# Changing the queues of the last stores, the prefetch of residual tiles and the start of the first products in a fused transformer block

## The chip, the cores and the metric

The kernel runs on one core of one Trainium2 chip. The metric is the device time of one execution, in microseconds (us). A timed value is that time. The span is the part of it that the profile covers, from the first instruction to the last, and is 1.6 to 2.2 us shorter. "Clock" is the mean clock granted to TensorE, as a share of full speed.

The engines are named as in the profile. PE is TensorE's matrix products and PEld its weight loads. DVE is VectorE, ACT is ScalarE, POOL is GpSimd and SP is SyncE. A "q" after the name means the engine's sequencer, which waits and issues transfers.

## The reference

The kernel computes one transformer block and all its gradients: linear attention (32 heads of 20), then a gated feed-forward network, each with a layer norm ahead and a residual. S is 2048, D 640 and F 1728, all in bf16.

```python
phi = lambda t: jnp.where(t > 0, t + 1, jnp.exp(t)) + 1e-6
q, k, v = ...                     # layernorm(x) @ wqkv, cut into heads
kv  = einsum("bhsd,bhse->bhde", phi(k), v)
z   = einsum("bhsd->bhd", phi(k))
o   = einsum(phi(q), kv) / (einsum(phi(q), z)[..., None] + 1e-6)
h   = x + o.reshape(B, S, D) @ wo
out = h + (silu(ln(h) @ w_gate) * (ln(h) @ w_up)) @ w_down
# returned: out, and the gradients for x, wqkv, wo, w_gate, w_up, w_down
```

## The kernel before

The token axis is cut into 16 tiles of 128 rows. The change touches three places.

**The start.** For every tile, VectorE makes the layer-norm statistics and the normalised tile `xn`. PE transposes that, ScalarE copies it out as `xnT`, PE multiplies it with the weights of k and q, ScalarE takes exp and relu, and VectorE makes phi of them.

```python
nc.sync.dma_start(out=x_tm[0][:, 0, 0:320], in_=x_v[:, 0, 0:320])
nc.scalar.dma_start(out=x_tm[0][:, 0, 320:640], in_=x_v[:, 0, 320:640])
load_x(nc.sync, 1, 2)
nc.sync.dma_start(out=wqk[:, :, D:2 * D], in_=...)       # k weights, one transfer of 800 KB
# after the statistics of tile 0: x tile 2, q weights, x tile 3
...
def kq_phi(t):
    for dst, e, r in ers.pop(t):
        nc.vector.tensor_scalar(out=e, in0=e, scalar1=1.0, scalar2=1e-6, op0=ALU.min, op1=ALU.add)
        nc.vector.tensor_tensor(out=half(dst[:, t, :]), in0=e, in1=r, op=ALU.add)
...
for t in range(ST):
    # t > 0:  normalise tile t+1, then k of tile t
    # t == 0: k of tile 0, then normalise tile 1
    ...                            # statistics of tile t+2
    kq_mm(t, 1)                    # q
    if t > 0:
        kq_phi(t - 1)
```

**The attention output.** Each tile reloads its residual `xr` on SyncE's queue in its own turn. Five transposed blocks of W2 go to memory on GpSimd's queue.

```python
xr = wk("xr")
nc.sync.dma_start(out=xr[:], in_=x_v[:, t, :])
... # products into ps_a, add, statistics, rstd on GpSimd
if 2 <= u <= DT + 1:
    nc.gpsimd.dma_start(out=mat_v(scr_W2T)[:, :, (u - 2) * P:(u - 1) * P], in_=w2t)
```

**The last stage.** Each of 16 tiles loads its `h1` rows on GpSimd's queue, adds the product with w_down, and stores the result on GpSimd's queue. Only the last tile's stores go by SyncE and ScalarE. The V part of the weight gradient (`dwv`, five stores) goes by GpSimd too.

```python
for t in range(ST):
    h1r = wk("h1r")
    nc.gpsimd.dma_start(out=h1r[:], in_=scr_h1_v[:, t, :])
    ...                                   # 28 products into ps_o
    nc.vector.tensor_tensor(out=half(h1r[:]), in0=row(ps), in1=half(h1r[:]), op=ALU.add)
    nc.gpsimd.dma_start(out=o0_v[:, t, :], in_=h1r[:])      # t < 15
    if t < DT:
        dwo(t); tr_sb(dKV, dKVT, t); tr_piece(Y, scr_Yt, t) # transposes on SyncE's queue
    if ST - 1 - DT <= t < ST - 1:
        dwv(t - (ST - 1 - DT))                              # store on GpSimd's queue
```

## Time and profile before

| | kernel before |
|---|---|
| time, median of 6 runs beside the changed kernel | 835.86 us (834.39 to 837.68) |
| profiled span, mean clock | 834.23 us, 0.996 |
| first k product starts | 7.87 us |
| z stage starts (after 16 tiles of k and q) | 57.28 us |
| PE's last product ends | 828.26 us |
| GpSimd's closing DRAIN | 825.47 to 833.45 us |

The table of windows and the timelines are the views that matter, because PE is busy 99% of the span. A part of the change can only be worth what PE stands still for in that place, or what comes after PE's last product. The rows are in the prediction below.

### The profile page before, as it was taken

Reading aid. Unit: us, or ns where it says so; the run is one execution under the profiler, and the core shown is the slowest. Engines: PE = TensorE matmul, PEld = TensorE weight load, DVE = VectorE, ACT = ScalarE, POOL = GpSimd, SP = SyncE. Lnnn points to the kernel's source line nnn. Section 1 sums busy time; section 2 is a strip of 40 time slices with the busy share of each in tenths; the row PEclk is TensorE's granted clock in tenths of the full one; section 3 lists DMA queues with packets and bytes.
Section 4 is the critical chain, followed back from the end, with each engine's and each line's share of the span. In section 5 each row is a group of like instructions: output and inputs, shape, how many; then the busy total and the mean of one; then the engine's idle time right before and its main releaser. Section 6 shows DMA issues by size and latency. Waiting matters only on the chain.

```text
span 834.2 us, 14051 instructions
## 1 busy us (share of the span) xinstructions
PE 823.7 (99%) x5523; PEld 529.3 (63%) x5523; DVE 446.1 (53%) x874; ACT 291.2 (35%) x414; POOL 197.2 (24%) x358
## 2 busy tenths in 40 slices
PE   8999999999999999999999999999999999999997
PEld 6776656555555555555656777777776777777775
DVE  6978757791087028810840158778864366611111
ACT  5983422670184125401830222232322133322000
POOL 2330132322312312221227102121301111112332
PEclk9999999999999999999999999999999999999999
DMA  9995899998559987993697758886698599899952
GB/s 290 184 353 127 166 162 253 278 237 199 145 130 213 211 196 167 202 234 89 123 267 176 248 145 197 198 199 161 165 196 141 106 179 158 158 244 194 278 154 80
DMA packets 277123, 158.55 MB, mean 190 GB/s; under 512 B 235760, under 2 KB 262960, under 8 KB 277056
## 3 DMA queue, kind: packets, MB, share of 16 engines
q1 hardware_dynamic: 250992, 80.48, 52.4%
q0 software_dynamic: 18688, 67.73, 26.6%
q10 hardware_dynamic: 7376, 9.44, 3.8%
q8 instruction: 43, 0.70, 0.4%
q14 instruction: 24, 0.20, 0.1%
HBM read 47.43 MB, written 53.46 MB: 121 GB/s over the span
## 4 chain that ended last, share of the span: by engine, by line
PE 86%; DVE 7%; DMA 3%; SPq 1%; ACT 1%; issue 1%; POOL 0%; ACTq 0%; DVEq 0%; POOLq 0%
PE ps_dw L558 20%; PE ps_dhn L116 14%; PE ps_dxn L792 8%; PE ps_o L845 7%; PE ps_kq L116 5%; PE ps_dwqk L116 5%; PE pg L486 4%; PE pu L491 4%; PE ps_y L116 3%; PE ps_gt L610 3%; PE ps_dk L116 3%; PE ps_dp L116 3%; PE ps_dm L328 2%; PE pdm L328 2%; DMA xr<-in_A_x_dram 1%; DVE m_s L513 1%
## 5 line engine op out<-in xcount | busy, mean ns | idle before, releaser
L116 PE MATMUL ps_dhn<-wgT,cols 128*128 128x320 bf16 x864 | 119.5, 299 | 0.0
L558 PE MATMUL ps_dw<-dd,hn 128*128 128x448 bf16 (+1 forms) x640 | 118.8, 346 | 0.0
L116 PEld LDWEIGHTS <-cols 128*128 128x128 bf16 x864 | 84.5, 98 | 32.9
L558 PEld LDWEIGHTS <-hn 128*128 128x128 bf16 x640 | 62.6, 98 | 54.2
L560 DVE CAST dwev<-ps_dw 128x896 bf16<-128x896 f32 (+3 forms) x12 | 10.9, 908 | 124.0 <-PE ps_dw L558 124.0
L523 POOL DMA_DIRECT2D scr_dT<-stg x64 | 34.7, 542 | 165.8 <-DMA stg<-dd 162.8
L560 ACT CAST dwev<-ps_dw 128x896 bf16<-128x896 f32 (+1 forms) x20 | 17.6, 879 | 158.3 <-PE ps_dw L558 158.3
L135 DVE CUSTOM_DVE_ANT_0 lb_a<-lb_dy,hn 128x640 bf16<-128x640 bf16 x32 | 26.4, 825 | 75.4 <-ACT lb_dy L133 75.4
L486 PE MATMUL pg<-wgu,hnT 128*128 128x448 bf16 (+1 forms) x320 | 63.6, 346 | 0.0
L491 PE MATMUL pu<-wgu,hnT 128*128 128x448 bf16 (+1 forms) x320 | 63.6, 346 | 0.0
L845 PE MATMUL ps_o<-wd,mT 128*128 128x320 bf16 (+2 forms) x462 | 62.7, 295 | 0.0
L558 PE MATMUL ps_dw<-m_s,dh 128*128 128x448 bf16 (+1 forms) x320 | 60.7, 346 | 0.4 <-DVE m_s L518 0.4
L792 PEld LDWEIGHTS <-ring 128*128 128x128 bf16 x480 | 46.9, 98 | 18.4 <-DMA ring<-dq 0.3
L845 PEld LDWEIGHTS <-mT 128*128 128x128 bf16 x462 | 44.5, 98 | 16.6
L792 PE MATMUL ps_dxn<-wqkvT,ring 128*128 128x320 bf16 x320 | 51.3, 299 | 0.0
L116 PE MATMUL ps_kq<-wqk,xnT 128*128 128x320 bf16 x320 | 47.5, 305 | 1.8 <-DMA wqk<-in_A_wqkv_dram 1.8
L558 PEld LDWEIGHTS <-dh 128*128 128x128 bf16 x320 | 31.3, 98 | 27.8 <-issue 0.9
L491 PEld LDWEIGHTS <-hnT 128*128 128x128 bf16 x320 | 31.3, 98 | 27.1
L486 PEld LDWEIGHTS <-hnT 128*128 128x128 bf16 x320 | 31.3, 98 | 27.1
L328 PEld LDWEIGHTS <-dh2T 128*128 128x128 bf16 x320 | 31.3, 98 | 25.1
L328 PE MATMUL ps_dm<-wdT,dh2T 128*128 128x448 bf16 (+1 forms) x240 | 46.9, 344 | 0.0
L133 ACT ACTIVATE lb_dy<-ps_dhn,rstd 128x640 bf16<-128x640 f32 x16 | 12.7, 794 | 87.4 <-PE ps_dhn L116 87.4
(161 smaller groups left out, 1300.6 us busy)
## 6 DMA issues: line engine op xcount, KB each, us to landing
scr_dT<-stg POOLq DMA_DIRECT2D x48, 224.0 KB, 3.3
cols<-scr_dT POOLq DMA_DIRECT2D x6, 1728.0 KB, 8.8
scr_m<-m_s POOLq DMA_DIRECT2D x12, 448.0 KB, 4.6
cols<-scr_dT ACTq DMA_DIRECT2D x2, 1728.0 KB, 9.0
out_dram<-dwev POOLq DMA_DIRECT2D x30, 112.0 KB, 2.1
scr_dT<-stg POOLq DMA_DIRECT2D x16, 192.0 KB, 3.4
scr_pk<-pk SPq DMA_DIRECT2D x4, 640.0 KB, 7.7
scr_pq<-pqa SPq DMA_DIRECT2D x4, 640.0 KB, 8.5
```

The costliest lines, as they stand in the source:

```text
L116: nc.tensor.matmul(ps[:, ci, :320], lhsT=lhs(k), rhs=rhs(k, n0, n1), start=(start and k == 0), stop=(stop and k == n - 1))
L133: nc.scalar.activation(out=half(dy[:]), in_=row(ps), func=ACT.Copy, scale=rstd_col, accum_out=sums[:, 0:1])
L135: nc.vector.tensor_tensor_reduce(out=a[:], in0=dy[:], in1=xhat, scale=1.0, scalar=0.0, op0=ALU.mult, op1=ALU.add, accum_out=sums[:, 1:2])
L328: nc.tensor.matmul(ps[:, c, :w], lhsT=dh2T[:, kt, (t + c) * P:(t + c + 1) * P], rhs=wdT[:, kt, o:o + w], start=(kt == 0), stop=(kt == DT - 1))
L486: nc.tensor.matmul(pg[:, c, :w], lhsT=hnT[:, kt, (t + c) * P:(t + c + 1) * P], rhs=wg[:, kt, 0:w], start=(kt == 0), stop=(kt == DT - 1))
L491: nc.tensor.matmul(pu[:, c, :w], lhsT=hnT[:, kt, (t + c) * P:(t + c + 1) * P], rhs=wg[:, kt, w:2 * w], start=(kt == 0), stop=(kt == DT - 1))
L523: nc.gpsimd.dma_start(out=scr_dT[t + c, :, KO[g]:KO[g] + GK[g], :], in_=stg[:, :GK[g], :])
L558: nc.tensor.matmul(ps[:, c, :w], lhsT=lhs(t), rhs=rhs(t), start=(t == 0), stop=(t == ST - 1))
L560: copy(out=ev[:, :len(parts), :w], in_=ps[:, :len(parts), :w])
L610: nc.tensor.matmul(ps[:, ci, :320], lhsT=dh1[:, t, i * P:(i + 1) * P], rhs=pqs_tm[:, t, n0:n1], start=(t == 0), stop=(t == ST - 1))
L792: nc.tensor.matmul(ps[:, ci, :320], lhsT=lhs[:, i, :], rhs=rhs[:, i, n0:n1], start=(k == 0 and i == 0), stop=(k == 2 and i == DT - 1))
L845: nc.tensor.matmul(po, lhsT=mT[:, t % 4, j, :], rhs=wd[:, j, n0:n1], start=(j == 0), stop=(j == FT - 1))
```

## The change

The intent is to start PE's work earlier, to keep loads ahead of their use, and to leave GpSimd's queue with nothing to do at the end.

```diff
@@ -109,12 +109,14 @@
     def bc(ap):
         return ap.unsqueeze(2).to_broadcast([P, H, Dh])
 
-    def mm_row(ps, lhs, rhs, n, start=True, stop=True):
-
-        for ci, (n0, n1) in enumerate(NCH):
-            for k in range(n):
-                nc.tensor.matmul(ps[:, ci, :320], lhsT=lhs(k), rhs=rhs(k, n0, n1),
-                                 start=(start and k == 0), stop=(stop and k == n - 1))
+    def mm_row(ps, lhs, rhs, n, start=True, stop=True, by_k=False):
+
+        steps = [(ci, k) for ci in range(2) for k in range(n)]
+        if by_k:
+            steps.sort(key=lambda x: x[1])
+        for ci, k in steps:
+            nc.tensor.matmul(ps[:, ci, :320], lhsT=lhs(k), rhs=rhs(k, *NCH[ci]),
+                             start=(start and k == 0), stop=(stop and k == n - 1))
 
     def ln_stats(src, mv):
         st6 = small.tile([P, 2, 6], FP32, name="st6", tag="st6")
@@ -184,8 +186,10 @@
 
     nc.sync.dma_start(out=x_tm[0][:, 0, 0:320], in_=x_v[:, 0, 0:320])
     nc.scalar.dma_start(out=x_tm[0][:, 0, 320:640], in_=x_v[:, 0, 320:640])
+    w_k = A_wqkv[:, D:2 * D].rearrange("(k p) n -> p k n", p=P)
+    nc.sync.dma_start(out=wqk[:, 0:3, D:2 * D], in_=w_k[:, 0:3, :])
     load_x(nc.sync, 1, 2)
-    nc.sync.dma_start(out=wqk[:, :, D:2 * D], in_=A_wqkv[:, D:2 * D].rearrange("(k p) n -> p k n", p=P))
+    nc.sync.dma_start(out=wqk[:, 3:5, D:2 * D], in_=w_k[:, 3:5, :])
 
     def wait_for(on, dmas):
         info = mybir.DependencyInfo(mybir.DependencyClass.Sync, mybir.DependencyReason.DATA)
@@ -265,19 +269,25 @@
     def kq_mm(t, which):
         dst, w0 = ((pk, D), (pqa, 0))[which]
         ps = mm("ps_kq")
-        mm_row(ps, lambda k: xnT[:, t, k, :], lambda k, n0, n1: wqk[:, k, w0 + n0:w0 + n1], DT)
-        e = fw("phi_e")
-        r = fw("phi_r")
-        nc.scalar.activation(out=e[:, :, :320], in_=row(ps), func=ACT.Exp)
-        nc.scalar.activation(out=r[:, :, :320], in_=row(ps), func=ACT.Relu)
-        ers.setdefault(t, []).append((dst, e, r))
-
-    def kq_phi(t):
-        for dst, e, r in ers.pop(t):
+        mm_row(ps, lambda k: xnT[:, t, k, :], lambda k, n0, n1: wqk[:, k, w0 + n0:w0 + n1], DT, by_k=(t == 0))
+
+        def act():
+            e = fw("phi_e")
+            r = fw("phi_r")
+            nc.scalar.activation(out=e[:, :, :320], in_=row(ps), func=ACT.Exp)
+            nc.scalar.activation(out=r[:, :, :320], in_=row(ps), func=ACT.Relu)
+            ers.setdefault(t, []).append((dst, e, r))
+
+        return act
+
+    def kq_phi(t, last=True):
+        n = len(ers[t]) if last else 1
+        for _ in range(n):
+            dst, e, r = ers[t].pop(0)
             nc.vector.tensor_scalar(out=e[:, :, :320], in0=e[:, :, :320], scalar1=1.0, scalar2=1e-6,
                                     op0=ALU.min, op1=ALU.add)
             nc.vector.tensor_tensor(out=half(dst[:, t, :]), in0=e[:, :, :320], in1=r[:, :, :320], op=ALU.add)
-        if t % 4 == 3:
+        if last and t % 4 == 3:
             sl = slice(t - 3, t + 1)
             nc.sync.dma_start(out=scr_pk_v[:, sl, :], in_=pk[:, sl, :])
             nc.sync.dma_start(out=scr_pq_v[:, sl, :], in_=pqa[:, sl, :])
@@ -286,22 +296,34 @@
     with tc.manual_schedule(engines={EngineType.PE, EngineType.DVE, EngineType.Activation}):
 
         ps = mm("ps_warm")
-        for _ in range(42):
-            nc.tensor.matmul(ps[:, 0, :P], lhsT=ident[:], rhs=ident[:], start=True, stop=True)
+
+        def warm(n):
+            for _ in range(n):
+                nc.tensor.matmul(ps[:, 0, :P], lhsT=ident[:], rhs=ident[:], start=True, stop=True)
+
+        warm(42)
         ln1_stats(0)
         ln1(0)
-        for t in range(ST):
-            if t > 0:
-                if t + 1 < ST:
-                    ln1(t + 1)
-                kq_mm(t, 0)
-            else:
-                kq_mm(t, 0)
+        warm(10)
+        act = kq_mm(0, 0)
+        ln1(1)
+        act()
+        ln1_stats(2)
+        kq_mm(1, 0)()
+        kq_mm(0, 1)()
+        for t in range(1, ST):
+            if t + 1 < ST:
                 ln1(t + 1)
+            if t == 2:
+                kq_phi(0)
+            if t > 1:
+                kq_mm(t, 0)()
             if t + 2 < ST:
                 ln1_stats(t + 2)
-            kq_mm(t, 1)
-            if t > 0:
+            if t == 1:
+                kq_phi(0, last=False)
+            kq_mm(t, 1)()
+            if t > 1:
                 kq_phi(t - 1)
         kq_phi(ST - 1)
 
@@ -390,6 +412,13 @@
         nc.vector.tensor_tensor(out=hb4(pq), in0=hb4(pq), in1=bc4(rall[:, t:t + 4, :]), op=ALU.mult)
         for tt in range(t, t + 4):
             nc.sync.dma_start_transpose(out=pqsT[:, :, tt * P:(tt + 1) * P], in_=pqa[:, tt, :])
+
+    xrs = {}
+
+    def load_xr(t):
+        if t < ST:
+            xrs[t] = wk("xr")
+            nc.sync.dma_start(out=xrs[t][:], in_=x_v[:, t, :])
 
     with tc.manual_schedule(engines={EngineType.PE, EngineType.DVE}):
         yk = strips.tile([P, 2, DT, D], BF16, name="yk", tag="S")
@@ -411,6 +440,8 @@
         dm(1)
         for t in range(0, 12, 4):
             normalise(t)
+        for t in range(3):
+            load_xr(t)
         for j in range(DT):
             d0, d1 = head_range(j)
             ps = mm("ps_kvt")
@@ -435,8 +466,7 @@
         h1s = {}
         for t in range(ST + 2):
             if t < ST:
-                xr = wk("xr")
-                nc.sync.dma_start(out=xr[:], in_=x_v[:, t, :])
+                xr = xrs.pop(t)
                 ps = mm("ps_a")
                 mm_row(ps, lambda i: pqsT[:, i, t * P:(t + 1) * P], lambda i, n0, n1: W2[:, i, n0:n1], DT)
                 nc.vector.tensor_tensor(out=half(xr[:]), in0=row(ps), in1=half(xr[:]), op=ALU.add)
@@ -446,11 +476,13 @@
                 ln_rstd(mv, rstd2, t, 1)
                 h1s[t] = (xr, mv)
                 dm(1)
+            if t > 0:
+                load_xr(t + 2)
             u = t - 2
             if u < 0:
                 continue
             if 2 <= u <= DT + 1:
-                nc.gpsimd.dma_start(out=mat_v(scr_W2T)[:, :, (u - 2) * P:(u - 1) * P], in_=w2t)
+                nc.sync.dma_start(out=mat_v(scr_W2T)[:, :, (u - 2) * P:(u - 1) * P], in_=w2t)
             if 1 <= u <= DT:
                 w2t = stage()[:, :DT, :]
                 nc.sync.dma_start_transpose(out=w2t, in_=W2[:, u - 1, :])
@@ -819,7 +851,7 @@
             nc.gpsimd.dma_start(out=out_3[j * P:(j + 1) * P, :], in_=ev[:])
 
         def dwv(i):
-            ev = wk("dwv")
+            ev = wk("dwv", pool=1)
             ps = mm("ps_dwv")
             for ci, (n0, n1) in enumerate(NCH):
                 ks = overlapping(n0, n1)
@@ -827,14 +859,23 @@
                     nc.tensor.matmul(ps[:, ci, :320], lhsT=Y[:, k, i * P:(i + 1) * P], rhs=dKV[:, k, n0:n1],
                                      start=(kk == 0), stop=(kk == len(ks) - 1))
             nc.scalar.copy(out=half(ev[:]), in_=row(ps))
-            nc.gpsimd.dma_start(out=out_2[i * P:(i + 1) * P, 2 * D:3 * D], in_=ev[:])
-
+            nc.scalar.dma_start(out=out_2[i * P:(i + 1) * P, 2 * D:3 * D], in_=ev[:])
+
+        h1rs = {}
+
+        def load_h1(t):
+            h1rs[t] = wk("h1r", pool=t % 2)
+            nc.gpsimd.dma_start(out=h1rs[t][:], in_=scr_h1_v[:, t, :])
+
+        for t in range(3):
+            load_h1(t)
         for t in range(ST):
             if t + MTA < ST:
                 load_mT(t + MTA)
+            if t + 3 < ST:
+                load_h1(t + 3)
             mT = mTs[t // 4]
-            h1r = wk("h1r")
-            nc.gpsimd.dma_start(out=h1r[:], in_=scr_h1_v[:, t, :])
+            h1r = h1rs.pop(t)
             ps = mm("ps_o")
             chs = NCH if t < ST - 1 else [(0, 320), (320, 512), (512, 640)]
             for ci, (n0, n1) in enumerate(chs):
@@ -849,11 +890,14 @@
                     (nc.sync, nc.scalar, nc.sync)[ci].dma_start(out=o0_v[:, t, n0:n1], in_=h1r[:, n0:n1])
             if t < ST - 1:
                 nc.vector.tensor_tensor(out=half(h1r[:]), in0=row(ps), in1=half(h1r[:]), op=ALU.add)
-                nc.gpsimd.dma_start(out=o0_v[:, t, :], in_=h1r[:])
+
+                (nc.gpsimd if t < 10 else nc.scalar).dma_start(out=o0_v[:, t, :], in_=h1r[:])
             if t < DT:
                 dwo(t)
-                tr_sb(dKV, dKVT, t)
-                tr_piece(Y, scr_Yt, t)
+            if 0 <= t - 3 < DT:
+                tr_sb(dKV, dKVT, t - 3)
+            if 0 <= t - 6 < DT:
+                tr_piece(Y, scr_Yt, t - 6)
             if ST - 1 - DT <= t < ST - 1:
                 dwv(t - (ST - 1 - DT))
 
```

## The prediction

> **What bounds the kernel now.** I read the page's busy row and chain first, to see which engine carries the time; then the table of windows, to find where that engine is not busy; then the timelines of those places.
>
> ```profile
> PE 823.7 (99%) x5523; PEld 529.3 (63%) x5523; DVE 446.1 (53%) x874; ACT 291.2 (35%) x414; POOL 197.2 (24%) x358
> PE 86%; DVE 7%; DMA 3%; SPq 1%; ACT 1%; issue 1%; POOL 0%; ACTq 0%; DVEq 0%; POOLq 0%
> ```
>
> TensorE is busy 823.7 us of a span of 834.2 us, and the change takes no matmul away; it adds ten small ones. So whatever the change does elsewhere, it can only win from the 10.5 us in which TensorE stands still, plus the time in which it runs at a lower clock. The windows say where those are (columns: window, length, then busy time and count of PE, PEld, DVE, ACT and POOL, granted clock, DMA share, GB/s):
>
> ```profile
> 4.60:8.00 3.40, 1.42 (x20) 1.14 (x19) 2.25 (x7) 0.48 (x1) 1.00 (x2) 1.00 1.03 343
> 8.00:11.40 3.40, 3.40 (x17) 2.13 (x16) 1.96 (x6) 0.77 (x2) 0.79 (x2) 0.50 1.05 371
> 14.00:57.00 43.00, 43.00 (x357) 31.99 (x355) 38.24 (x107) 42.94 (x73) 16.33 (x30) 1.00 1.06 265
> 100.00:119.00 19.00, 18.41 (x112) 10.84 (x111) 7.04 (x15) 4.53 (x5) 6.35 (x11) 1.00 0.89 153
> 760.00:820.00 60.00, 60.00 (x444) 43.24 (x442) 11.55 (x14) 6.19 (x10) 19.34 (x36) 1.00 0.85 195
> 830.20:834.20 4.00, 0.00 (x0) 0.00 (x0) 0.00 (x0) 0.00 (x0) 0.00 (x0) 0.55 0.00 0
> ```
>
> Three places lose time. Between 4.6 and 8.0 us TensorE works 1.42 us, and in the next 3.4 us its clock is granted at 0.50. Around 100 to 119 us it misses 0.59 us. After 830.2 us nothing at all runs for 4 us and no byte moves. The last stage (760 to 820 us), to which most lines of the change belong, has TensorE busy 60.00 of 60.00 us: its loads and stores have no time to give.
>
> The timeline of the start shows the first gap:
>
> ```profile
> 5.59 0.45 PE L256 MATMUL ps_t<-ident,xn 128*128 128x128 bf16 x5
> 7.87 2.72 PE L116 MATMUL ps_kq<-wqk,xnT 128*128 128x320 bf16 x10 [1.83 <-DMA wqk<-in_A_wqkv_dram]
> 10.92 1.78 PE L116 MATMUL ps_kq<-wqk,xnT 128*128 128x320 bf16 x10
> ```
>
> The transposes of tile 0 end at 6.04 us, then TensorE waits 1.83 us for the 800 KB of k weights, and its first ten matmuls take 2.72 us. In the chain of the stage that follows, twenty of the same shape take 2.72 us, so ten should take 1.36 us: the halved clock cost another 1.36 us.
>
> The end, from SyncE's own waits in 820 to 834 us:
>
> ```profile
> SPq L884 <- PEq L884: 3.9, 2, 3.4
> ```
>
> The last store has landed at 830.1 us; SyncE then waits up to 3.4 us in the closing barrier. PE is named, but PE ended at 828.3 us. In the trace's records the one that comes last is a DRAIN instruction on GpSimd: it starts at 825.47 us, beside GpSimd's last store, and takes 7.98 us, until 833.45 us; the barrier opens at 833.5 us and the program ends at 834.2 us.
>
> **What the Trainium skill says.** "TensorE: Matmul & The Clock Gate", Part 1, has the clock halved after an idle window of about 3.4 us and says the window runs freely, so that its phase differs from run to run. The trace agrees: one window of 3.4 us at 0.50, just after one in which PE was busy 42%. "DMA: Bandwidth & Descriptors", section "Issuing engines are not separate DMA queues", says that issuing from other engines saves only sequencer time. The trace has that saving: a GpSimd issue of these stores takes 540 ns, one on ScalarE 330 to 360 ns. So I expect no faster transfer. "VectorE: DVE Perf Modes", section "The DRAIN you can't avoid", gives the DRAINs of a program's start and end as a constant 12 ns or so. Here the GpSimd one took 7.98 us; the measurement decides.
>
> **The change part by part.** I compared the order of the instructions on each engine in both builds.
>
> *The head.* The k weights come as 480 KB ahead of x tile 1 and 320 KB behind it; the first ten matmuls go by k block over both halves, so the first six need only the first piece; ten warm-up matmuls fill the gap; and k of tile 1 is computed before q of tile 0. Before, x tile 0 landed at 3.25 us, tile 1 at 3.61, and the k weights at 6.1 to 7.8: thirteen of the sixteen DMA engines were done by 6.64 us, the last at 7.83. The bytes are the same in another order, at some 340 KB/us. My estimates are that the first piece lands at 4.5 to 5.5 us, x tile 1 at 5 to 5.8, the second piece at 6.5 to 7.5. The transposed tile 0 is ready at 6.56 us (its first three blocks) and about 7.0 (the rest). So k of tile 0 starts near 6.6 instead of 7.87 us, after ten warm-up matmuls of some 56 ns, and ends near 8.0 to 8.4 instead of 10.59 us, if the clock holds. In the window 4.6 to 8.0 us PE would then be busy 0.84 (warm-up) + 0.45 (transposes) + 0.56 (new warm-up) + about 1.1 (k), near 2.9 of 3.4 us; I take it that the clock stays at 1.00.
>
> Not all of that 2.2 us is kept. K of tile 1 needs xnT of tile 1, whose chain is: VectorE's normalised tile ready at 7.88 us, transposes to 8.4, ScalarE's copy (0.70 us) to 9.2. So PE pauses about 0.8 us, runs k of tile 1 to 10.6 us, q of tile 0 to about 11.9 and the transposes of tile 2 to about 12.2 us. The q weights landed at 10.5 us before, so they are just in time. Before, the same set of work (k0, q0, k1 and two transposes) was done at 12.97 + 1.36 = 14.33 us. PE is ahead by 2.1 us. But in this stage ScalarE is as full as PE (42.94 of 43 us): five passes a tile at a pitch of 0.60 us make 3.0 us, PE's period too. Its account: by 13.8 us it will have done eight passes, where before it had done six by 14.49 us: 0.69 + 2 x 0.60 = 1.9 us ahead. I keep the smaller, less a little for the start of the steady state: **1.8 us**.
>
> *The middle.* The x tiles are prefetched in the program text, but the order on SyncE is the old one: all five buffers were already loaded ahead. What moves is the five W2 stores, from GpSimd to SyncE. Before, GpSimd waited 19.6 us in all for the transposed W2 tiles ahead of its layer-norm work, and through that VectorE and then PE stood still: PE 0.59 us at 118.3. On SyncE the stores wait behind the same transposes, five issues of about 0.45 us, and delay the later hnT transposes by 1 to 2 us; those are used from 149 us on. Worth **0.6 us**, perhaps less.
>
> *The last stage.* h1 tiles three ahead, transposes later, the dwv stores and the h1 stores of tiles 10 to 14 on ScalarE's queue. PE had no wait there, so this is worth nothing while the stage runs. What it changes is GpSimd's last work: it becomes the store of tile 9 (evacuated at 802 us) and the last h1 load, so the DRAIN begins near 804 to 806 and ends, if it takes 8 us again, near 814 us, far ahead of the end. The barrier then waits for the last store: 830.22 instead of 833.5 us, **3.3 us**.
>
> Sum: 1.8 + 0.6 + 3.3 = 5.7 us; 835.81 - 5.7 = 830.1 us.
>
> **The rivals.** (a) The DRAIN is not a matter of where GpSimd ends but waits for all DMA or has work of its own until the end; then the tail stays 3.3 us longer: 833.4 us. For it: the DRAIN outlasted the last landing. Against it: it outlasted the last landing by 3.4 us, while nothing moved. (b) The clock is throttled in the head all the same, because the free-running window falls badly or because PE's new pause counts: 1.4 us lost, 831.5 us. (c) Moving x tile 1 behind 480 KB makes it late: VectorE does its statistics ahead of the copy of tile 0's last blocks, so each us of lateness goes straight into the first matmuls; the head then gains 0.5 us: 831.4 us. (d) The later transposes of dKV and Y, or the SyncE queue with W2 stores in it, make PE wait where it did not: plus 1 to 3 us, 831 to 833 us. PE's slack there is four tiles of about 4.6 us, so I give it little. (e) More than I count: without a throttled window and with the weights early, 828 us.
>
> **Range and chances.** All these are a few us; runs of the kernel before spread over 3 us. I predict 830.1 us, with 827.8 to 833.0 us for 8 in 10. A difference of 2% is 16.7 us, more than all the idle time of TensorE, so faster by over 2% has 0.01, slower 0.01, within 2% 0.98.
>
> **What would show it right or wrong.** The head: the clock at 1.00 from 8 to 11.4 us, the first k matmuls before 7 us, ten of them in about 1.4 us, PE's first q stage over 1.5 to 2 us earlier. The middle: no PE wait near 118 us. The tail: SyncE's wait in the closing barrier under 0.5 us instead of 3.4, and the span ending within 2.5 us of VectorE's last instruction instead of 5.6. PE's busy time in the last stage unchanged. A new PE wait anywhere after 14 us, or a DRAIN that still ends last, would make it wrong.

## The result, and the profile after

The changed kernel takes 832.13 us (median of 6 runs, 831.13 to 832.78), the kernel before 835.86 us in the same rounds. The ratio is 0.995 with a 95% interval of 0.9935 to 0.9966: 0.5% faster, which is "within 2%". A ratio here is the mean time of one kernel's fast runs over the mean of the other's fast runs of the same rounds, so it is not quite the ratio of the medians.

The profiled span is 830.49 us against 834.23 us, 3.74 us less. The busy row of the page:

```profile
PE 823.2 (99%) x5533; PEld 527.7 (64%) x5533; DVE 446.4 (54%) x874; ACT 291.8 (35%) x414; POOL 187.4 (23%) x343
```

PE has ten products more and POOL fifteen instructions less, as the diff says. These are the windows of the changed kernel, with the same columns as in the prediction:

```profile
4.60:8.00 3.40, 2.97 (x36) 2.07 (x34) 1.89 (x6) 0.48 (x1) 0.89 (x2) 1.00 0.98 316
8.00:11.40 3.40, 2.42 (x20) 1.49 (x19) 1.90 (x5) 1.91 (x4) 0.82 (x3) 1.00 1.04 336
14.00:57.00 43.00, 42.25 (x347) 29.97 (x346) 38.68 (x108) 42.28 (x71) 16.14 (x30) 1.00 1.09 278
100.00:119.00 19.00, 19.00 (x118) 11.39 (x117) 10.57 (x23) 5.44 (x6) 3.75 (x10) 1.00 0.88 173
760.00:820.00 60.00, 60.00 (x444) 43.22 (x442) 11.55 (x14) 6.22 (x9) 15.04 (x28) 1.00 1.04 196
830.20:834.20 4.00, 0.00 (x0) 0.00 (x0) 0.00 (x0) 0.00 (x0) 0.00 (x0) 0.68 0.00 2
```

The clock holds at 1.00 in the start and PE is busy 2.97 of 3.40 us there, as predicted. The wait at 118 us is gone (19.00 of 19.00). The window of 14 to 57 us is new: PE lost 0.75 us in it, where before it lost nothing. The last row has no work left to show, because the span ends at 830.49.

The timeline of PE at the start:

```profile
5.51 0.45 PE L260 MATMUL ps_t<-ident,xn 128*128 128x128 bf16 x5 [0.28 <-DVE xn L256]
6.53 1.84 PE L118 MATMUL ps_kq<-wqk,xnT 128*128 128x320 bf16 x10
8.58 0.45 PE L260 MATMUL ps_t<-ident,xn 128*128 128x128 bf16 x5 [0.20 <-DVE xn L256]
9.81 2.89 PE L118 MATMUL ps_kq<-wqk,xnT 128*128 128x320 bf16 x20 [0.78 <-ACT xnT L267]
18.27 0.45 PE L260 MATMUL ps_t<-ident,xn 128*128 128x128 bf16 x5 [0.61 <-DVE xn L256]
```

K of tile 0 starts at 6.53 instead of 7.87 us. Then PE has to wait for tile 1, and at 18.27 us once more, for the normalised tile 4. All of PE's waits between 0 and 60 us (columns: total us, times, longest), first of the kernel before:

```profile
PE ps_kq L116 <- DMA wqk<-in_A_wqkv_dram: 1.8, 1, 1.8
PE ps_warm L290 <- POOL ident masks.py:199: 1.4, 1, 1.4
```

and of the changed kernel:

```profile
PE ps_warm L302 <- POOL ident masks.py:199: 1.4, 1, 1.4
PE ps_t L260 <- DVE xn L256: 1.1, 3, 0.6
PE ps_kq L118 <- ACT xnT L267: 0.8, 1, 0.8
```

The wait for k's weights, 1.8 us, has become waits of 1.1 us for VectorE and 0.8 us for ScalarE's copy, 1.9 us together, of which the prediction had counted on 0.8. The z stage, which follows all k and q products, starts at 57.26 us, against 57.28. In this pair of profiles PE's lead is 1.34 us at the first k product, 0.24 us at the first k product of tile 3 (18.56 against 18.80 us), and 0.02 us at the z stage. SyncE's closing waits, from 815 to 834 us:

```profile
SPq L928 <- PEq L928: 0.7, 2, 0.5
SPq L928 <- DMA out_dram<-h1r: 0.6, 1, 0.6
```

The barrier's wait has shrunk from 3.4 to 0.5 us. The sum of the differences between the two profiles, counted from the starts of stages:

| stretch | before | after | gained |
|---|---|---|---|
| start to z stage | 57.28 | 57.26 | 0.02 |
| z stage to the first weight-gradient product of the network | 125.52 | 124.77 | 0.75 |
| from there to PE's last product | 645.46 | 645.71 | -0.25 |
| PE's last product to the end | 5.97 | 2.75 | 3.22 |
| span | 834.23 | 830.49 | 3.74 |

Part of the 0.25 us shows at the head of that stretch: the page's row of the weight-gradient products waits 0.8 us on VectorE's `m_s`, against 0.4 before.

```profile
L590 PE MATMUL ps_dw<-m_s,dh 128*128 128x448 bf16 (+1 forms) x320 | 60.7, 346 | 0.8 <-DVE m_s L550 0.8
```

### The profile page after: what moved, and what is told of

It is laid out like the page before. It is cut to its first block, busy times and chain, and to the rows that moved or that the text cites. A ratio compares the mean times of both kernels' runs of the same rounds, so it can differ in the third digit from the quotient of the medians.

```text
span 830.5 us, 14069 instructions
## 1 busy us (share of the span) xinstructions
PE 823.2 (99%) x5533; PEld 527.7 (64%) x5533; DVE 446.4 (54%) x874; ACT 291.8 (35%) x414; POOL 187.4 (23%) x343
## 4 chain that ended last, share of the span: by engine, by line
PE 87%; DVE 8%; DMA 3%; ACT 1%; issue 1%; POOL 0%; SPq 0%; ACTq 0%; DVEq 0%
PE ps_dw L590 20%; PE ps_dhn L118 14%; PE ps_dxn L824 8%; PE ps_o L886 7%; PE ps_dwqk L118 5%; PE ps_kq L118 4%; PE pg L518 4%; PE ps_dm L350 4%; PE pu L523 4%; PE ps_y L118 3%; PE ps_gt L642 3%; PE ps_dp L118 3%; PE ps_dk L118 3%; PE pdm L350 2%; PE ps_a L118 2%; DMA xr<-in_A_x_dram 1%
## 5 line engine op out<-in xcount | busy, mean ns | idle before, releaser
L892 DVE TENSOR_TENSOR h1r<-ps_o,h1r 128x640 bf16<-128x640 f32 x15 | 12.4, 825 | 56.6 <-PE ps_o L886 46.7
```

## The experiments

Two questions are open. Why is nothing of the head left at the z stage of the profile, when its first product starts 1.3 us earlier? And which part makes the end shorter? Twelve kernels were run, each on one chip beside the kernel before (834 to 841 us there). Two give a wrong result (e5 and e6); the others are correct.

| run | median (range), us | before, median | ratio (95%) |
|---|---|---|---|
| e1_stores_back | 831.76 (831.51 to 832.96) | 837.65 | 0.9933 (0.9910 to 0.9955) |
| e2_queues_only | 834.11 (833.28 to 836.18) | 837.65 | 0.9961 (0.9939 to 0.9983) |
| e3_one_late_store | 830.80 (830.47 to 832.02) | 837.65 | 0.9923 (0.9902 to 0.9944) |
| e4_old_head | 833.16 (831.63 to 834.79) | 837.65 | 0.9948 (0.9926 to 0.9970) |
| e5_q_phi_cut (wrong result) | 830.77 (830.28 to 832.32) | 837.14 | 0.9926 (0.9897 to 0.9955) |
| e7_q_phi_gpsimd | 864.22 (863.23 to 865.97) | 837.14 | 1.0318 (1.0284 to 1.0353) |
| e8_x3_first | 832.01 (831.78 to 832.63) | 837.14 | 0.9939 (0.9911 to 0.9966) |
| e10_tail_undone | 832.58 (831.86 to 833.81) | 837.14 | 0.9946 (0.9917 to 0.9975) |
| e9_w2_stores_back | 835.82 (834.74 to 837.34) | 836.73 | 0.9986 (0.9957 to 1.0014) |
| e6_old_head_q_phi_cut (wrong result) | 832.61 (831.44 to 833.17) | 836.73 | 0.9944 (0.9917 to 0.9971) |
| e11_x1_x3_first | 831.85 (831.54 to 832.52) | 836.73 | 0.9936 (0.9905 to 0.9966) |
| e12_tail_as_before | 831.96 (831.84 to 832.31) | 836.73 | 0.9939 (0.9913 to 0.9965) |

The parts are worth a few us at most, so I compare profiles, and times only within one call. A profile is one execution, and need not be a typical one: those of e4 and e10 are the fastest run of their kernel, 831.63 and 831.86 us.

### The end of the program

Four runs change the last stores. In e1, all of them go back to GpSimd's queue, while the h1 tiles stay prefetched:

```diff
-            nc.scalar.dma_start(out=out_2[...], in_=ev[:])                         # dwv
+            nc.gpsimd.dma_start(out=out_2[...], in_=ev[:])
-                (nc.gpsimd if t < 10 else nc.scalar).dma_start(out=o0_v[:, t, :], in_=h1r[:])
+                nc.gpsimd.dma_start(out=o0_v[:, t, :], in_=h1r[:])
```

> The changed kernel with the stores of h1 (tiles 10 to 14) and of dwv back on GpSimd's queue; everything else as changed. Theory (the program ends when GpSimd's closing DRAIN does, 6.6 to 8.0 us after GpSimd's last DMA issue): the last issue returns to about 825 us, the DRAIN ends near 833, SyncE's wait in the closing barrier is over 3 us again and the time is some 3.2 us above the changed kernel, about 835.3 us. Rival (the gain came from the head and the middle of the kernel): the time stays below 833 us.

In e2, the kernel before gets those two new queues and nothing else (the same diff, the other way round):

> The kernel before with the store queues alone changed (h1 of tiles 10 to 14 and dwv on ScalarE's queue). GpSimd still loads h1 of the last tile late, near 821.6 us, so its DRAIN ends at 828.2 to 829.6 us by the theory, before the last store has landed at about 830.1: the tail's 3.3 us are won by this part alone, time about 832.6 us. Rival (the tail needs the earlier h1 loads, or the other parts bring the gain): over 834 us.

In e3, the changed kernel gets one single late store, that of tile 14, on GpSimd's queue:

```diff
-                (nc.gpsimd if t < 10 else nc.scalar).dma_start(out=o0_v[:, t, :], in_=h1r[:])
+                (nc.scalar if 10 <= t < ST - 2 else nc.gpsimd).dma_start(out=o0_v[:, t, :], in_=h1r[:])
```

> The changed kernel with one store alone, h1 of tile 14, back on GpSimd, issued near 824 us. Theory (a DRAIN of 6.6 to 8 us from GpSimd's last DMA issue, however many there are): it ends at 830.7 to 832.1 us where the barrier otherwise opens at 829.7, so 1 to 2.3 us longer than the changed kernel. Rival (the DRAIN grows with the number of GpSimd's late stores, ten of them before): 0.3 us or less.

In e10, the h1 loads go back to their own turn too, and only the later place of the transposes and the alternating buffers are kept:

```diff
-        for t in range(3):
-            load_h1(t)
...
-            if t + 3 < ST:
-                load_h1(t + 3)
+            load_h1(t)
... # and both lines of e1
```

> The changed kernel with both parts of the tail undone: the h1 tiles loaded in their own turn again, and the last stores of the first output and of the V weight gradient back on GpSimd's queue. Either part alone kept the gain (the closing DRAIN ended at 829.8 with the prefetch alone and at 826.4 with the queues alone). Theory A (either part suffices because each lets GpSimd reach its DRAIN about 2 us sooner or shortens it): here the DRAIN begins at about 824.9 and lasts about 8 us, ends at 832.5 to 833, and the kernel loses 2.5 to 3.2 us: a span of about 833. Theory B (the tail's gain comes of something else, such as the later transposes on SyncE's queue, which are kept here): the DRAIN ends before 830.5 and the span stays within 0.8 us of the changed kernel's.

These gave an answer against my theory. GpSimd's late work was back in e1, e3 and e10, and the barrier opened only 0.05 to 1.2 us later for it, not 3.2: a program end of 3.62, 2.80 and 3.98 us after PE's last product, against 2.75 in the changed kernel and 5.97 before. The DRAIN was simply shorter than before, 4.9 to 5.6 us instead of 7.98. E2 went the other way: the two queues alone brought the end from 5.97 to 3.09 us, with the DRAIN over at 826.40 us, but its time, 834.11 us, missed the 832.6 expected (in its profile the first k product started 0.4 us later than in the kernel before, and the attention output waited 1.2 us instead of 0.6). The theory that the whole gain of the end is where GpSimd's last store stands had failed, and its rival, the place of the transposes, was tried by e12, which has the whole last stage of the kernel before:

```diff
 # e10, and in addition
-            ev = wk("dwv", pool=1)
+            ev = wk("dwv")
-            h1rs[t] = wk("h1r", pool=t % 2)
+            h1rs[t] = wk("h1r")
-            if 0 <= t - 3 < DT:
-                tr_sb(dKV, dKVT, t - 3)
-            if 0 <= t - 6 < DT:
-                tr_piece(Y, scr_Yt, t - 6)
+                tr_sb(dKV, dKVT, t)
+                tr_piece(Y, scr_Yt, t)
```

> The changed kernel with the whole last stage of the kernel before: stores, h1 loads, buffers and the place of the transposes. With the transposes left late, undoing the rest cost only some 1.2 us. Theory A (the transposes or buffers are the missing part): the DRAIN lasts about 8 us as in the kernel before and ends 5.2 us after TensorE's last matmul, for a span of 832.3 to 833.3. Theory B (the DRAIN's rest goes with the number of transfers on GpSimd's queue, 282 here and 287 in the kernel before, or merely varies): it ends 3.4 to 3.5 us after the last landing and some 3.0 us after the last matmul, and the span is 830 to 831.

With the last stage exactly as it was, the program ends 3.90 us after PE's last product, not 5.97. (The expected 3.0 was missed: the DRAIN did end 2.82 us after that product, but the program 1.08 us after the DRAIN, where it was 0.78 in the kernel before; what held it is not known.) SyncE's closing waits of e12, from 820 to 834 us:

```profile
SPq L923 <- PEq L923: 1.7, 2, 1.2
SPq L923 <- DMA out_dram<-h1r: 0.7, 2, 0.6
```

The longest wait is 1.2 us; in the kernel before it is 3.4, in the changed kernel 0.5. So 2.07 of the 3.22 us came from outside the last stage. What differs in the program outside it and touches GpSimd is the five W2 stores, 700 us earlier. No run moved them alone in the kernel before, so that they are the cause of the 2.07 us is inferred, from single profiles. Counting the transfers that each program issues on GpSimd's queue gave the following table; the rest is the time from the last landing of any of them to the end of the closing DRAIN, from the trace's records:

```text
transfers  kernel           DRAIN starts  takes   rest after last landing   program's end after PE's last product
   272     changed             802.51     6.56        2.13                      2.75
   272     e4, e5, e6, e8, e11 801 to 803   5.0-6.4      2.13 (all five)           2.73 to 3.01
   272     e7                  836.62     4.80        2.28                      2.73
   273     e3                  823.85     4.88        2.79                      2.80
   277     e2                  819.24     7.17        4.70                      3.09
   277     e9                  807.10     7.19        4.56                      3.04
   282     e1                  824.16     5.62        3.49                      3.62
   282     e10                 823.52     5.62        3.41                      3.98
   282     e12                 823.88     5.62        3.49                      3.90
   287     before              825.47     7.98        5.89                      5.97
```

Programs with the same count have the same rest to within 0.15 us, and whether the last transfers are early or late doesn't change it. The test of this was e9, in which the five W2 stores alone go back to GpSimd's queue. Its expectation was on record before it ran:

```diff
-                nc.sync.dma_start(out=mat_v(scr_W2T)[:, :, (u - 2) * P:(u - 1) * P], in_=w2t)
+                nc.gpsimd.dma_start(out=mat_v(scr_W2T)[:, :, (u - 2) * P:(u - 1) * P], in_=w2t)
```

> The changed kernel with the five stores of the transposed W2 alone back on GpSimd's queue. If these stores made TensorE's wait at 118 us, it is back: the attention output stage takes 43.8 us or more instead of 43.2, and TensorE's last matmul comes 0.4 to 0.6 us later for the same head. It also makes 277 transfers on GpSimd's queue instead of 272. In six profiles with 272 the closing DRAIN ended 2.1 to 2.3 us after the last of them landed; with 273, 277, 282, 282 and 287 it took 2.8, 4.7, 3.5, 3.4 and 5.9. If the count of the queue's transfers sets this rest, it is about 4.7 here, though the tail is untouched; if what happens late on the queue sets it, it stays at 2.1. The time is not touched by that either way, because this DRAIN begins at about 802.

The rest came to 4.56 us, against 2.13 with the stores on SyncE, though not one line of the last stage differs. The count is therefore what goes with it, and not in proportion: 277 has more than 282. In the trace GpSimd's transfers take eight semaphores in turn, and the remainder of the count by eight (0, 1, 2, 5, 7) does put the rests in rising order (2.13, 2.79, 3.4 to 3.5, 4.6 to 4.7, 5.89). That the DRAIN has to do something for each of these is only my reading; no run shows it.

E9 brought a second answer that I had not expected. Its time is 835.82 us, beside 831.85 and 831.96 for e11 and e12, and the ranges do not touch. The middle itself lost 0.36 us: the attention output took 50.22 us (from 101.37 us on) against 49.87 in the changed kernel and 50.61 in the kernel before (51.27 in e2, which has the old middle too), 0.2 us of it a wait of ps_a. (The lengths of 43.2 and 43.8 us in the expectation are those of the stage ahead of it, a mistake.) The rest is at 622 us. PE's waits from 455 to 650 us, of which the changed kernel and the kernel before have none:

```profile
PE ps_wv L118 <- DVE hn L751: 2.6, 1, 2.6
PE ps_wv L118 <- DMA wqkvT<-in_A_wqkv_dram: 0.4, 1, 0.4
```

VectorE is named, but is not the cause: in the changed kernel the same product starts at 624.0 us, 2.2 us before that VectorE instruction. Here it starts at 625.84, just after the third of the transposed weights `wqkvT` that it needs has landed at 625.71 (614.0 in the changed kernel). They came late together with reloads of xnT on GpSimd's queue, of which the last three landed at 620.0 to 625.3 us instead of 608.9 to 612.8. The windows of e9, same columns as above:

```profile
618.00:625.00 7.00, 5.11 (x73) 3.77 (x71) 2.85 (x8) 0.69 (x1) 0.00 (x0) 1.00 1.43 72
625.00:632.00 7.00, 5.77 (x22) 3.05 (x23) 6.39 (x18) 2.08 (x3) 0.00 (x0) 0.51 0.87 140
```

After the wait the clock is granted at 0.51 for 7 us, which costs some 2.7 us more (from this product to PE's last one 206.48 us pass, in the changed kernel 203.76). The other three runs of e9 were not profiled. Two of them have clock 1.000 and spans of 832.7 and 833.5 us, 2 to 3 us over those of e11 and e12, so the wait is probably there without the half clock. Why moving five stores at 100 to 115 us should make reloads at 600 us late is open, and so is whether it does: in e1 and e12, which have these stores on SyncE, the last reload landed at 618.1 and 616.7 us, also late, and PE did not wait. GpSimd issues the second of those four reloads 1.75 us after the first in e9, and 0.75 us after it in the changed kernel; but the kernel before has the 1.75 us too and no late landing in its profile.

### The start

In e4, the changed kernel has the start of the kernel before (loads, order and warm-up as in the first four hunks of the diff, undone):

> The changed kernel with the head of the kernel before: one load of the k weights behind x tile 1, no second warm-up, q of tile 0 after k of tile 0. Theory (VectorE paces the k and q stage, so the head's lead is given back before the stage ends): ps_z starts within 0.2 us of 57.3 us as in both kernels, time within 0.4 us of the changed kernel. Rival (my prediction: the head is worth 1.8 us): ps_z and the end come 1.5 to 2 us later than in the changed kernel. The clock in 8 to 11.4 us should be at half again.

In e5, VectorE is relieved: q's tensor_scalar is left out, a wrong result. E6 makes the same cut in e4, so with the old start.

```diff
-            nc.vector.tensor_scalar(out=e[:, :, :320], in0=e[:, :, :320], scalar1=1.0, scalar2=1e-6,
-                                    op0=ALU.min, op1=ALU.add)
+            if dst is pk:
+                nc.vector.tensor_scalar(out=e[:, :, :320], in0=e[:, :, :320], scalar1=1.0, scalar2=1e-6,
+                                        op0=ALU.min, op1=ALU.add)
```

> The changed kernel with one VectorE instruction per token tile (the tensor_scalar of q's feature map, sixteen in all) taken out; the result is wrong on purpose. Theory A (VectorE paces the k/q stage at 3.015 us a tile, so the head's early start is lost to VectorE's chain): a tile then costs VectorE some 0.3 us less, the next pacer (PE at about 2.99 us, ScalarE near it) takes over, and the first matmul of the z stage comes at 56.2 or earlier instead of 57.26; the kernel gains about 1 us on 832.1. Theory B (ScalarE or PE bounds the stage, as the prediction said): the z stage still starts at 57.2 to 57.3 and the time stays.

> The changed kernel with the head of the kernel before and q's tensor_scalar taken out on VectorE (wrong on purpose), to stand beside the same cut with the new head, whose z stage started at 55.64 (first k product at 6.68). If TensorE is what paces once VectorE is relieved, then the head's early start is worth its full length here: the z stage starts 49.0 us after the first k product, so at 56 if k's weights land at 7 and at 57.2 if they land at 8.2. If the order of VectorE's instructions is what counts, the z stage starts at 55.6 or sooner whenever the first k product comes.

In e7, the same sixteen instructions go to GpSimd, so the result is right:

```diff
-            nc.vector.tensor_scalar(out=e[:, :, :320], ...
+            (nc.vector if dst is pk else nc.gpsimd).tensor_scalar(out=e[:, :, :320], ...
```

> The changed kernel with the same sixteen instructions moved to GpSimd, so the result stays right. Theory A: the z stage starts about 1 us earlier (56.3 or so) if GpSimd does one in under 2 us; if GpSimd is slower than that[...], VectorE's later half of the map waits for it and the stage gets longer, 58 or more. Theory B: no move.

In e8, x tile 3 is asked for ahead of q's weights; e11 has this, and x tile 1 ahead of k's first piece too:

```diff
 # e8
     yield load_x(nc.sync, 2, 3)
+    yield load_x(nc.sync, 3, 4)
     yield nc.sync.dma_start(out=wqk[:, :, 0:D], in_=...)
-    yield load_x(nc.sync, 3, 4)
 # e11, in addition
+    load_x(nc.sync, 1, 2)
     nc.sync.dma_start(out=wqk[:, 0:3, D:2 * D], in_=w_k[:, 0:3, :])
-    load_x(nc.sync, 1, 2)
```

> The changed kernel with x tile 3 asked for ahead of q's first weights instead of behind them. Theory A, with the start of the statistics of tile 3 (11.61, held by the landing of x tile 3) as what sets VectorE's chain: the statistics of tile 3 start at about 9.5, xn of tile 4 about 16.5 instead of 17.77, and the z stage starts about 1 us earlier, unless q's weights now come later than 11.5 and hold q of tile 0, which the mapping of VectorE's order would turn into the same wait. Theory B: nothing moves but the waits of VectorE.

> The changed kernel with x tile 1 ahead of k's first piece and x tile 3 ahead of q's weights, result unchanged: a try at a better kernel. If VectorE paces and is held by x tiles 1 and 3, the statistics of tile 1 start at about 5.3 instead of 6.09, those of tile 3 at about 9.7 instead of 11.61, and the z stage at 55.6 to 56.0 instead of 57.26, for 1.3 to 1.6 us less than the changed kernel's profiled time; but k's second piece lands 0.4 us later and may hold the first k product to 7.1, which would give 56.3. If ScalarE or TensorE paces, only the start of the first k product counts and the z stage comes at 57.3 or later.

What the profiles show of the start, all in us from the start of the span (a transfer has landed when the slowest of the sixteen DMA engines is done):

```text
kernel    start  x1 landed  q weights  x3 landed  first k  stats tile 3  xn tile 4  z stage
before    old      3.61      10.52      10.96      7.87      10.99        17.49     57.28
e2        old      3.65      11.00      11.45      8.29      11.47        17.37     57.16
e4        old      3.65       9.47       9.89      6.79      10.12        15.84     55.64
e6 (cut)  old      3.62      11.37      11.81      8.12      11.83        17.72     57.53
changed   new      6.06      11.15      11.58      6.53      11.61        17.77     57.26
e10       new      5.86       9.59      10.04      6.98      10.72        16.88     56.37
e12       new      5.45       9.62      10.07      7.26      10.33        17.11     56.59
e9        new      5.55      10.19      10.63      7.41      10.65        17.25     56.74
e5 (cut)  new      5.48      10.07      10.52      6.68      10.54        16.25     55.64
e8        x3 first 5.67      10.77       7.74      7.05      10.53        16.91     56.39
e11       both     4.57      12.35       8.05      7.44      10.45        18.27     57.77
```

Three things can be read from it. First, the same programs move by 1 us and more between profiles with the landing of the same loads: the old start reached the z stage at 55.64, 57.16 and 57.28 us. E4 is such a lucky one: its k weights landed at 6.75 us where the kernel before had 7.83. So a comparison of single profiles, as I had made it between before and after, is good to 1 us here and no better.

Second, in the profiles the new start is not ahead by the z stage. Over six profiles (changed, e1, e3, e9, e10, e12) the z stage starts at 56.37 to 57.26 us, mean 56.88 (e1 and e3, not in the table, had 57.16 each). Over the three with the old start (before, e2, e4) the mean is 56.70. The new order costs something too: in every profile with it VectorE stands still 0.46 us ahead of xn of tile 3, for GpSimd's rstd, and in none with the old one.

The times say otherwise. E4 differs from the changed kernel in the start alone. Its six runs have a mean of 833.20 us, beside 831.97 for e1 and 831.09 for e3: 1.2 and 2.1 us longer, with a standard error of about 0.5 us each. E6 has 832.46 beside 831.03 for e5, on the same chip, 1.4 us longer. They were run at other times. The profile of e4 is the fastest of its six runs; the other five have spans 0.8 to 3.2 us longer, and no trace of them is kept. So in e4 the theory (time within 0.4 us) missed in time, both sides missed in the profile (55.64 us, no halved clock), and in time the rival, a head worth 1.8 us, is the nearer. A part may lie elsewhere: e4's profile, alone of all, has a PE wait of 0.9 us in the last stage, at 767 us. What the head is worth stays open, from nothing to some 2 us.

Third, VectorE holds the steady part of the changed kernel. Its timeline in the changed kernel over one whole tile:

```profile
29.83 0.44 DVE L256 TENSOR_SCALAR xn<-x_tm,mv,rstd 128x640 bf16<-128x640 bf16 x1
30.19 0.88 DVE L124 BATCH_NORM_STATS2 st<-x_tm 128x6 f32<-128x320 bf16 x2
31.10 0.21 DVE L125 BATCH_NORM_AGGREGATE mv<-st 128x2 f32<-128x12 f32 x1
31.23 0.27 DVE L287 TENSOR_SCALAR phi_e<-phi_e 128x640 bf16<-128x640 bf16 x1
31.61 0.49 DVE L289 TENSOR_TENSOR pk<-phi_e,phi_r 128x640 bf16<-128x640 bf16 x1
32.02 0.32 DVE L287 TENSOR_SCALAR phi_e<-phi_e 128x640 bf16<-128x640 bf16 x1
32.44 0.49 DVE L289 TENSOR_TENSOR pqa<-phi_e,phi_r 128x640 bf16<-128x640 bf16 x1
32.85 0.44 DVE L256 TENSOR_SCALAR xn<-x_tm,mv,rstd 128x640 bf16<-128x640 bf16 x1
```

No row has a bracket with an idle time: the engine goes from one instruction to the next for 3.02 us, tile after tile. The window of 14 to 57 us calls it busy only 38.68 of 43 us, because the busy time leaves out the gaps of 0.03 to 0.11 us between instructions that follow each other without a wait. That is what I had overlooked. The pitch is 3.016 us in the kernel before too. The waits from 14 to 57 us say the same; in the changed kernel PE's weight loads wait for VectorE's tile again and again:

```profile
PEld L260 <- DVE xn L256: 3.4, 13, 0.9
DVE phi_e L287 <- ACT phi_e L277: 0.5, 2, 0.3
DVE pqa L289 <- ACT phi_r L278: 0.3, 1, 0.3
```

The kernel before has no such wait of PE's weight loads. There k and q of one tile follow those of the last at 2.995 us, and VectorE's xn at 3.015 us, so VectorE began ahead and lost 0.02 us a tile; xn of tile 15 comes 6.62 us before the z stage, where in the changed kernel it comes 6.31 us before it. The earlier start of PE has used up that reserve, and VectorE has become the engine that paces. This pace explains only the last 0.22 us of the lost lead; the rest was gone by tile 3. With VectorE relieved (e5) it is VectorE that waits for ScalarE instead:

```profile
DVE pqa L290 <- ACT phi_r L278: 4.2, 12, 0.7
DVE phi_e L288 <- ACT phi_e L277: 1.3, 3, 0.7
```

In e5 the z stage starts at 55.64 us, 1.6 us sooner than in the changed kernel, of which 0.4 to 0.7 us may be relief (0.73 us against e10, whose first k product is 0.30 us later) and the rest its earlier loads. In time e5 is 1.1 us under e8, by the means. From tile 7 on VectorE's xn follow each other at 2.996 us instead of 3.016. The pitch falls no further, because ScalarE comes next: all three engines lie within 1% of each other. With the cut, the old start gives 57.53 us (e6) and the new one 55.64, so there the new start shows, with the reserve that e6's loads were slow ones; I had expected 57.1 from its first product at 8.12 us, and it came 0.4 us later, held by q's weights at 11.37 us.

GpSimd was no help (e7). In its timeline and waits (14 to 57 us):

```profile
45.52 2.37 POOL L287 TENSOR_SCALAR phi_e<-phi_e 128x640 bf16<-128x640 bf16 x1
```

```profile
DVE pqa L289 <- POOL phi_e L287: 20.3, 8, 2.9
```

One instruction takes 2.37 us there against 0.32 on VectorE, and the next tile's rstd stands behind it on the same engine, so a tile takes 5.6 us, and the kernel 32 us more than the changed one.

E8 and e11 show what reordering the loads gives: nothing that holds. With x tile 3 at 7.74 us, its statistics start at 10.53 us, not at the 9.5 I expected, since they follow the normalised tile 2, which starts at 10.17. In e11 q's weights landed at 12.35 us and held the first q products: the hold moved from one load to another. Neither is faster than the changed kernel in time (832.01 and 831.85 against 832.13, in other calls), and no tried version with a right result clearly beats it; e3, with 830.80, is within what chips and rounds differ by.

One thing the new start seems to give is an even clock. Of 16 runs with the old start (e2, e4, e6), six had a mean clock below 1.000, down to 0.997. Of 38 with the new one (changed, e1, e3, e5, e8, e10, e11, e12; e7 and e9 have long waits of their own), six had 0.999 and none less; of those, the two profiled (e10, e12) have their half-clock window after PE's last product. Of the 25 runs of the kernel before, 24 were below 1.000, down to 0.994, but they have a longer end too, at a clock of 0.55 in the profile.

## Why the prediction was right and where it was wrong

The predicted time was 830.1 us with a range of 827.8 to 833.0; measured were 832.13 us, so the range and the class held, with 3.7 us of the 5.7 gained (4.1 by the means). E1, e3, e8 and e11, which differ from the changed kernel by the queue or the order of a few transfers, gained 5.1 to 6.5 us by the means. They were run at other times. So the missing 2 us are within what calls differ by.

**The head (1.8 us predicted; 0.02 in the pair of profiles, 1.2 to 2.1 by the times of the experiments).** The events came as predicted: clock 1.00, k at 6.53 us, PE 2.97 us busy in the first window. In the profile, what failed is the step "in this stage ScalarE is as full as PE", which took ScalarE for the engine whose lead is kept. VectorE is as full as either (3.016 us a tile against 2.995). It gained no lead, since x tile 1 landed at 6.06 instead of 3.61 us behind k's first piece, and x tile 3, behind q's weights, at 11.58 instead of 10.96: xn of tile 4 came at 17.77 us, 0.28 us later than before. That is rival (c), with its mechanism. VectorE's copy of tile 0's last blocks, first before and then after the change:

```profile
6.68 0.28 DVE L261 COPY xnT<-ps_t 128x256 bf16<-128x256 bf16 x1
7.32 0.28 DVE L265 COPY xnT<-ps_t 128x256 bf16<-128x256 bf16 x1
```

The first k matmuls waited for it, so that ten took 1.84 us and not 1.4. I had put what remains in this case at 0.5 us; the profile has none left by the z stage. And the halved clock, for which I counted 1.36 us, cost the kernel before about 0.5 us: its z stage starts 49.41 us after its first k product, those of e2 and e4, with no halved window, 48.87 and 48.85. Whether the 1.8 us were wrong as a mean over runs is open, since the times of e4 and e6 agree with them.

**The middle (0.6 us predicted).** In the profiles it was 0.75 us, with 0.25 us given back later; the wait at 118 us is gone. The step was right for its place. What it may have missed is that the five stores matter elsewhere. With them back (e9), the time is 3.9 us longer than e11 and e12, in the one profile mostly by a wait at 622 us. Whether such waits are part of the unprofiled runs of the kernel before is open; its one profile has none.

**The end (3.3 us predicted, 3.22 measured).** Both the size and the immediate cause were right, and e2 shows that the predicted way, the stores' queue alone, is worth 2.88 us: the barrier no longer waits for GpSimd's DRAIN (3.4 to 0.5 us). The step "becomes the store of tile 9 and the last h1 load, so the DRAIN begins near 804 to 806" came at 802.51 us. But the DRAIN's 8 us is not a constant, as "if it takes 8 us again" allows. The last stage of before, put into the changed kernel (e12), ends 3.90 us after PE and not 5.97. Thus 2.07 us of the 3.22 come, as far as can be inferred, with the five W2 stores that had left GpSimd's queue 700 us earlier, and the last stage's own lines are then worth the other 1.15 us. The two overlap: with all W2 stores left where they were (e9), the new last stage alone brings the end to 3.04 us.

**The rivals.** (a), a DRAIN with work of its own, was half right: it has 2.1 to 5.9 us of it after the last landing, but begins early enough now. (b), the clock, did not come. (d), new waits from the later transposes or SyncE's queue, did not come: the last stage is busy 60.00 of 60.00 us. (e) did not come.

**The signs.** The clock, the first k product, the wait at 118 us, SyncE's wait (0.5 us) and the end (2.42 us after VectorE's last instruction, instead of 5.64) came as named. PE's first q products came no earlier (11.19 against 10.92 us; they stand behind k of tile 1 now). One that was named as a sign of being wrong came too, "a new PE wait anywhere after 14 us": 0.61 us at 18.27 us, for VectorE, and 0.4 us more at `m_s`.

## What to carry to other kernels

When several engines are within 2% of a stage's period, a head start on one of them can be lost, as in the profile here, unless the fullest one gets it too; judge fullness by the timeline, where instructions follow without idle brackets, not by busy time alone. Look at what ends last after the last useful product: here it was GpSimd's closing DRAIN, and taking five transfers off GpSimd's queue 700 us earlier shortened it (e9 against the changed kernel), though not in proportion to their number. Compare starts only over several profiles, because landings of the same loads move by 1 us, and hold them against the times of all runs: the one profile kept may be the fastest run.

## What the Trainium skill lacked or had wrong

- "VectorE: DVE Perf Modes", section "The DRAIN you can't avoid", gives the runtime's DRAINs at a program's beginning and end as about 12 ns each and constant. (The ones here are recorded at the kernel's last line; whether the page means these too is not shown.) In the last barrier those of SyncE, ScalarE, VectorE and TensorE do take 0.01 to 0.02 us in the changed kernel. In the barrier before it ScalarE's took 0.15 us, VectorE's 0.33, TensorE's 1.30, and GpSimd's 4.8 to 8.0 us in fourteen profiles.
- No page says what GpSimd's closing DRAIN depends on. Here its rest after the last landing followed the number of transfers on GpSimd's queue: 2.1 to 2.3 us with 272, 2.79 with 273, 4.6 to 4.7 with 277, 3.4 to 3.5 with 282, 5.89 with 287. Why is open.
- No page gives how far apart the sixteen DMA engines finish one transfer. For q's weights in the changed kernel the thirteenth was done at 9.44 us and the last at 11.15, before GpSimd had issued any transfer (its first came at 53.1 us). Which engines lagged was not read.
- "Trainium Architecture — The Big Picture", section "The five engines, in one table", has GpSimd 2 times slower than VectorE at streaming elementwise work. A tensor_scalar of 128x640 bf16 took 2.37 us on it and 0.32 on VectorE, 7 times as long.
- "TensorE: Matmul & The Clock Gate", Part 1, has the clock fall after an idle window of about 3.4 us, and windows of 3.4 us are what the traces show. The window need not be idle altogether: the clock was halved after windows in which PE was busy 42% (before, 4.6 to 8.0 us) and 44% (e9, 621.7 to 625.1 us), and kept after one of 46% (e2, 6.1 to 9.5 us), but also after one of 42% (e7, 44.96 to 48.37 us, 1.45 of 3.41 us). So the busy share that the traces give doesn't draw the line; what does is not shown.
